# Fused scan and two MLPs on one core: the first two weight tiles in half-batches, a written-out order for the first block, attention loads on another queue

## Chip, cores, metric

The kernel runs on one core of a Trainium2 chip. The metric is the device time of one execution in microseconds (us); the outputs go back to HBM within it. Three runs of the kernel before gave 627.05, 629.52 and 629.43 us (median 629.43). One more execution, 627.23 us long, was recorded by the profiler; all rows below come from it.

## What is computed

```python
def _attn_ref(x, a, B, C):        # x (4, 8, 768, 32), a (4, 8, 768), B and C (4, 8, 768, 16)
    log_a = np.log(np.clip(a, 1e-06, 1.0))
    for c in range(nc):           # chunks along the sequence
        cum = np.cumsum(la, axis=-1)
        L = causal * np.exp(cum[:, :, :, None] - cum[:, :, None, :])
        M = np.einsum('bhin,bhjn->bhij', Cc, Bc) * L
        y[:, :, sl] = M @ xc + (Cc @ state) * np.exp(cum)[..., None]
        state = decay_full * state + sum_j(Bc x xc * decay_from_j)

def _moe_ref(x, w_gate, w_val, w_out, rms_g):       # x (3072, 256), d_ff 1536
    xn = x / np.sqrt(np.mean(x * x, axis=-1, keepdims=True) + 1e-06) * rms_g
    g = xn @ w_gate
    return (g / (1.0 + np.exp(-g)) * (xn @ w_val)) @ w_out

def _moe2_ref(x, w_in, w_out):                      # d_ff 2048
    h = x @ w_in
    return (h * np.clip(h + 3.0, 0.0, 6.0) / 6.0) @ w_out
```

A decayed linear attention over 4 batches feeds a normalised gated MLP, whose output feeds a second MLP. The MLP weights come in 64-bit floats, everything else in 32-bit.

## The kernel before, in words

**Tiles.** The sequence is cut into 6 blocks of 128 positions. A block holds the 4 batches: 4 "chunks" of 128 columns, 512 columns in all. Chunks are worked in pairs, q = 0 to 11; pairs 0 and 1 are the first block. Phase A runs the first MLP: 6 blocks times 12 weight tiles (`step`, f = 0 to 11). Phase B runs the second: 6 blocks times 16 weight tiles. Every product of two numbers is made from a high and a low part, as three matmuls (`mm3`, L829): high·high, low weight·high, high weight·low. So a step of phase A is two `hidden` groups of 6 matmuls of 512 columns (into `hps`), a `gate` on ScalarE (Silu, L862), a `prod` on VectorE (L870), a split into `gh` (ScalarE, L877) and `gl` (VectorE, L257), and one `result` group of 6 matmuls into `acc`. Two `hps` tiles and three each of `p`, `gh`, `gl` are in use in turn.

**Weights.** `weights` loads a tile of 64-bit numbers (768 KB) and turns it into `w1h` and `w1l`: two ScalarE passes (L772, L777), a VectorE join (L781), a cast to the high part (L261 or L263) and a VectorE subtraction (L257, `w1l`). Six staging buffers (`raw`) are used in turn. Every tile after the first also has a `hold`: a one-column GpSimd copy into the staging buffer (L975), which makes the tile's load wait for something earlier (`um` of chunk 1, or an earlier tile).

**Attention.** For each pair: loads of `cb` (all of C, B and x), of `L` (decays, spread to 64 partitions) and of `P` (prefix products); a VectorE scan of `L` (L454), products `bh` and `ch` (L257), then on TensorE `score` (L481) and `grow` (L492), on VectorE `SM` (L534), `um` (L540) and the state `V` (L548), then `intra` (L506) and `inter` (L515). ScalarE squares the result (L576). In the first block `L` and `P` are spread from SBUF by matmuls (L358, L364) with one-hot matrices `pick` and `eyeN`, which ScalarE copies out of the identity `eye` (L373, L379); GpSimd makes `eye8` and `eye`, in that order (L275 to L283). The norm of the first block is done for each pair (`norm_pair`): a mean by matmul (L597), a Sqrt on ScalarE (L629), a Newton step on VectorE (L610 to L612), a spread by matmul (L637), the scaling (L642) and the split of x into `xh` and `xl`. Later blocks use `norm` (L691 to L717), with a round trip through HBM (`rnd`, `rb`). Scores, products and sums of a pair lie in one PSUM tile, `sps`.

**Order.** Nothing is in program order. `Plan` collects operations with guessed durations, dependencies (`r`, `w`), pure order (`seq`) and a `boost`; `run` then simulates the engines and, whenever one is free, gives it the ready operation with the longest remaining path plus boost. Instructions are issued in the order so found, on one in-order queue for each engine. The place of an operation in the list decides only which buffers follow which. The first MLP step waits for all four batches (`xkeys[0]`). From the last mean of the first block until that step, `fill` puts matmuls on zeros (`idle`, L325) into gaps of TensorE, and `heat` runs six passes on zeros at the start (L351). All loads but four small or early ones go out on SyncE's queue (SP): weights (L763), `L` (L415), `cb` (L409), `P` (L424), the round trip of the norm (L709, L713).

Of the kernel before, what the change touches and what calls it, by code (L numbers as in the profile page):

```python
# [30 lines left out]
NWARM = (4, 4, 2)  # L31
VISITS = {0: [(0, 2, None), (2, 3, 2), (6, None, 3), (8,)],
# [3 lines left out]
class Plan:  # L36
# [9 lines left out]
    SLACK, BIAS = 400, 600  # L46
# [3 lines left out]
    def __init__(self, bufs):  # L50
        self.bufs, self.ops = bufs, []
        self.last, self.readers, self.users, self.first = {}, {}, {}, {}
        self.fill, self.pace, self.bytes, self.calm = None, {}, {}, 0

    def op(self, ns, fn, r=(), w=(), boost=0, seq=()):

        i, deps, order = len(self.ops), set(), set()
        ns = dict(ns)
        if "bytes" in ns:
            self.bytes[i] = ns.pop("bytes")  # L60
# [23 lines left out]

    def run(self):
# [22 lines left out]
        done, left, out = set(), set(), []  # L108
# [9 lines left out]
        while len(out) < len(ops):  # L118
# [21 lines left out]
            pri, i = now[e][0]  # L140

# [20 lines left out]
            if e == "POOL":  # L162
                free["DVE"] = max(free["DVE"], t) + self.SHARE * ops[i][0][e]
            land = end + self.LAT[e]
            if i in self.bytes:
                pipe = max(pipe, end) + self.bytes[i] / self.RATE
                land = pipe + self.LAND
            out.append((t, i, e))
            for s, full in succ[i]:
# [4 lines left out]
        out = [(t, i, lambda i=i, e=e: ops[i][1](e), ops[i][0][e] if e == "PE" else None)  # L174
               for t, i, e in out]
        if self.fill:
            fn, ns, after, cold, until = self.fill
            t = 1 + max(s for s, i, _, _ in out if i in after)
            cold += t
            for s, i, _, pe in sorted(o for o in out if o[3] is not None):  # L180
                while t + ns + self.SLACK < s:
                    out.append((t, -1, fn, None))
                    t += ns if t > cold else 2 * ns
                if i == until:
                    break
                t = max(t, s + pe)
# [5 lines left out]
def block_kernel(ctx, tc, comb, ablk, w1, w2, cst, out):  # L192
# [18 lines left out]
    ps_at = att.enter_context(tc.tile_pool(name="ps_at", bufs=1, space=PSUM, side="right"))  # L211
    ps_q = early[0].enter_context(tc.tile_pool(name="ps_q", bufs=1, space=PSUM))
# [15 lines left out]
    T = {}  # L228
# [6 lines left out]
    def dma(nbytes, n=1, e="DMA"):  # L235
        return {e: max(560 * n, nbytes // 370) if e == "DMA" else 560 * n, "bytes": nbytes}
# [32 lines left out]
    def setup():  # L269
# [4 lines left out]
        dve.memset(ac[:, 4], 1.0)  # L274
        pool.memset(eye8, 0.0)  # L275
        for base in (0, SC):
# [3 lines left out]
        pool.memset(ah, 0.0)  # L280
        pool.memset(eye, 0.0)
        pool.affine_select(out=eye, in_=eye, pattern=[[1, 128]], compare_op=ALU.not_equal,
                           fill=1.0, base=0, channel_multiplier=-1)  # L283

    P.op({"POOL": 2800}, lambda e: None, w=[("eye", 0)], boost=1e9)
# [12 lines left out]
    def clip_all(e):  # L298
        dve.tensor_scalar(out=az, in0=ac, scalar1=1e-6, scalar2=1.0, op0=ALU.max, op1=ALU.min)
        dve.tensor_copy(ah[:, :, 0:1], az[:, :, 0:1])  # L300
        dve.memset(az[:, :, 0:1], 0.0)
# [9 lines left out]
    def prefixes():  # L311
        P.op({"DVE": d2(320) + 280}, clip_all, r=[("ac", 0), ("ac", 1), ("eye", 0)], w=[("az", 0)], boost=1e5)
        P.op(dma(98304), lambda e: nc.sync.dma_start(out=rows(azero), in_=az[:, :4]), r=[("az", 0)],
             w=[("azero", 0)], boost=2e5)
        P.op({"DVE": ds(320)}, prefix, r=[("az", 0)], w=[("ac", 0), ("ac", 1)], boost=1e5)
# [8 lines left out]
    def idle():  # L324
        pe.matmul(out=bank4()[:, 0], lhsT=zero, rhs=four(zero), start=True, stop=True)  # L325


# [3 lines left out]
    def bank4(k=0):  # L331
        if ("ps", 0) not in T:
            T["ps", 0] = ps_at.tile([128, 4, 512], F32, name="sps")
        return T["ps", 1 if 2 <= k < B else 0]

    SCORE, Y, U = (0, 128), (256, 64), (384, 64)

# [756 lines left out]
```

## Time and profile before

| | |
|---|---|
| median of 3 runs (lowest, highest) | 629.43 us (627.05, 629.52) |
| profiled execution | 627.23 us |
| its span | 625.2 us |
| outside the span | 2.03 us |
| busy: TensorE, weight loads, VectorE, ScalarE, GpSimd | 610.8, 494.6, 388.5, 297.3, 6.9 us |

PE is TensorE, PEld its weight loads, DVE VectorE, ACT ScalarE, POOL GpSimd, SP SyncE; a "q" behind a name is that engine's queue of DMA issues. A busy time that is nearly the span names the busiest engine, not what each stage waits for; that is read from views of short stretches.

### The profile page before, as it was taken

The numbers are of one execution on the slowest core, as the hardware profiler recorded it, in microseconds if no ns is written. First come the engines' busy times: TensorE is split into PE (matmuls) and PEld (weight loads), VectorE is DVE, ScalarE is ACT, GpSimd is POOL, SyncE is SP. The second block draws the span as 40 slices with busy tenths as digits, with TensorE's granted clock in tenths as the row PEclk, the third lists the DMA queues.
The fourth block names the chain that finished last, engine by engine and source line by source line (L and its number), as shares of the span: only waits on it lengthen the run. The fifth ranks groups of instructions, "written<-read, shape, count | busy, mean of one in ns | idle before, by whom it ended". The sixth has DMA issues, their size and how long they took to land.

```text
span 625.2 us, 10728 instructions
## 1 busy us (share of the span) xinstructions
PE 610.8 (98%) x4442; PEld 494.6 (79%) x4442; DVE 388.5 (62%) x703; ACT 297.3 (48%) x501; POOL 6.9 (1%) x21
## 2 busy tenths in 40 slices
PE   7898999999999999999999999999999999999997
PEld 5576888788788778788888888888888888888886
DVE  6799988853793585566875455555555546454554
ACT  3687723232333323346765345454445445444543
POOL 1000000000000000000000000000000000000000
PEclk9799999999999999999999999999999999999999
DMA  5899205300420310023441000000000000000000
GB/s 199 312 240 332 71 18 144 106 15 18 145 61 0 103 61 17 2 91 129 147 150 41 1 0 1 1 35 1 1 35 0 0 35 1 18 17 0 35 1 35
DMA packets 15017, 40.89 MB, mean 65 GB/s; under 512 B 2084, under 2 KB 4856, under 8 KB 14968
## 3 DMA queue, kind: packets, MB, share of 16 engines
q1 hardware_dynamic: 14488, 39.24, 19.3%
q10 hardware_dynamic: 480, 0.96, 0.4%
q8 instruction: 35, 0.57, 0.4%
q14 instruction: 14, 0.11, 0.1%
HBM read 36.84 MB, written 3.35 MB: 64 GB/s over the span
## 4 chain that ended last, share of the span: by engine, by line
PE 91%; DVE 4%; DMA 3%; ACT 1%; issue 1%; SPq 0%; DVEq 0%
PE hps L829 48%; PE acc L829 36%; DMA cb<-comb 2%; DVE SM L534 1%; PE sps L506 1%; PE sps L481 1%; PE sps L515 1%; DMA P<-pref 1%; PE spread L351 1%; PE sps L492 1%; DVE L L454 1%; ACT sq L576 1%; PE sps L691 1%; PE spread L358 0%; DVE um L540 0%
## 5 line engine op out<-in xcount | busy, mean ns | idle before, releaser
L877 ACT CAST gh<-p 128x512 fp32r<-128x512 f32 x168 | 104.2, 621 | 149.8 <-PE acc L829 148.7
L257 DVE TENSOR_TENSOR gl<-p,gh 128x512 fp32r<-128x512 f32 x168 | 115.5, 688 | 78.0 <-ACT gh L877 77.9
L872 DVE SCALAR_TENSOR_TENSOR p<-p,hps 128x512 f32<-128x512 f32 x96 | 66.0, 688 | 71.9 <-ACT p L864 71.8
L864 ACT ACTIVATE p<-hps,half 128x512 f32<-128x512 f32 x96 | 66.1, 689 | 72.0 <-DVE gl L257 71.9
L829 PE MATMUL hps<-xh,w1h 128*128 128x512 f32 x288 | 90.7, 396 | 1.2 <-DVE p L870 0.7
L829 PE MATMUL hps<-xh,w1l 128*128 128x512 f32 x288 | 89.2, 391 | 0.5 <-DVE w1l L257 0.5
L829 PE MATMUL hps<-xl,w1h 128*128 128x512 f32 x288 | 88.8, 390 | 0.0
L829 PE MATMUL acc<-gh,w2h 128*128 128x512 f32 x192 | 74.7, 389 | 0.0
L829 PE MATMUL acc<-gh,w2l 128*128 128x512 f32 x192 | 74.7, 389 | 0.0
L829 PE MATMUL acc<-gl,w2h 128*128 128x512 f32 x192 | 74.7, 389 | 0.0
L870 DVE TENSOR_TENSOR p<-p,hps 128x512 f32<-128x512 f32 x72 | 49.3, 685 | 35.0 <-PE hps L829 27.6
L862 ACT ACTIVATE p<-hps 128x512 f32<-128x512 f32 x72 | 43.0, 597 | 48.4 <-DVE gl L257 24.8
L829 PEld LDWEIGHTS hps<-xh,w1h 128*128 128x128 f32 x288 | 52.9, 188 | 14.3 <-DVE p L870 1.3
L829 PEld LDWEIGHTS hps<-xh,w1l 128*128 128x128 f32 x288 | 53.8, 188 | 13.0 <-DVE w1l L257 1.7
L829 PEld LDWEIGHTS hps<-xl,w1h 128*128 128x128 f32 x288 | 54.0, 188 | 11.7 <-issue 0.2
L829 PE MATMUL hps<-xh,w2l 128*128 128x512 f32 x192 | 59.1, 389 | 0.0
L829 PE MATMUL hps<-xl,w2h 128*128 128x512 f32 x192 | 59.1, 389 | 0.0
L829 PE MATMUL hps<-xh,w2h 128*128 128x512 f32 x192 | 59.1, 389 | 0.0
L829 PE MATMUL acc<-gh,w1h 128*128 128x512 f32 x144 | 56.5, 392 | 0.0
L829 PE MATMUL acc<-gh,w1l 128*128 128x512 f32 x144 | 56.1, 389 | 0.0
L829 PE MATMUL acc<-gl,w1h 128*128 128x512 f32 x144 | 56.0, 389 | 0.0
L829 PEld LDWEIGHTS acc<-gh,w2l 128*128 128x128 f32 x192 | 36.0, 188 | 7.5
(106 smaller groups left out, 638.7 us busy)
## 6 DMA issues: line engine op xcount, KB each, us to landing
cb<-comb SPq DMA_DIRECT2D x10, 896.0 KB
raw<-w SPq DMA_DIRECT2D x16, 512.0 KB
L<-azero SPq DMA_DIRECT2D x20, 256.0 KB
yT<-w SPq DMA_DIRECT2D x6, 768.0 KB
rawx<-w SPq DMA_DIRECT2D x6, 768.0 KB
out<-yT SPq DMA_DIRECT2D x12, 256.0 KB
P<-pref SPq DMA_DIRECT2D x20, 64.0 KB
rb<-rnd SPq DMA_DIRECT2D x5, 256.0 KB
```

The lines of the kernel that those rows point to most:

```text
L257: eng[e].tensor_tensor(out=out, in0=a, in1=b, op=op)
L351: pe.matmul(out=Q[3][:, :128 * n], lhsT=zero, rhs=four(zero, n), start=True, stop=True)
L454: dve.tensor_tensor_scan(out=L, data0=Q[k] if k < B else L, data1=flat(eye8), initial=0.0, op0=ALU.mult, op1=ALU.add)
L481: pe.matmul(out=o[64 * c:64 * c + 64, p], lhsT=cb[r, BN + c * SC:BN + (c + 1) * SC], rhs=cb[r, CP + c * CH:CP + (c + 1) * CH], start=True, ...
L492: pe.matmul(out=o[32 * p:32 * p + 32, c], lhsT=b[r, 32 * p:32 * p + 32], rhs=cb[r, XX + 64 * p:XX + 64 * p + 64], start=False, stop=True, ...
L506: pe.matmul(out=y[32 * g:32 * g + 32, 2 * t + c], rhs=SM[r, h], lhsT=cb[r, XX + D * h:XX + D * h + D], start=first, stop=True, skip_group_ ...
L829: pe.matmul(out=o, lhsT=a, rhs=c, start=first and i == 0, stop=last and i == len(seq) - 1)
L862: act.activation(out=p[:, :n], in_=hid(hs[0])[:, :n], func=AF.Silu)
L864: act.activation(out=p[:, :n], in_=hid(hs[0])[:, :n], func=AF.Relu, scale=1.0 / 6.0, bias=half)
L870: dve.tensor_tensor(out=p, in0=p, in1=h, op=ALU.mult)
L872: dve.scalar_tensor_tensor(out=p, in0=p, scalar=1.0, in1=h, op0=ALU.min, op1=ALU.mult)
L877: act.copy(out=t[:, :n], in_=T["p", i][:, :n])
```

## The change

- The first two weight tiles (`NE = 2`) are run for the first block in two half-batches of 256 columns: batches 0 and 1 (pair 0) with f = 0 and 1, then batches 2 and 3 (pair 1) with f = 0 and 1; from f = 2 on all 512 columns as before. In a half step both hidden groups share one `hps` tile. A gate now also waits for the Silu table.
- `chain` writes out the order of the first block on VectorE, ScalarE and TensorE.
- `spot` and `each` go from ScalarE to VectorE; GpSimd makes `eye` first; `heat` makes two matmuls (four passes) where it made three; `fill` and `idle` are gone.
- `L`, `cb` and `P` of all pairs from 2 on are issued by GpSimd. Only f = 3 keeps a `hold` (on `um` of chunk 3); later tiles come after it in order.
- `sps` tiles are marked (`ps=`), so that the planner keeps an engine off one that another engine still uses; the two PSUM pools swap places, so that the first pair's tile is freed first.
- The `VISITS` of block 0 move down the list; some guessed durations change.

```diff
-NWARM = (4, 4, 2)
-VISITS = {0: [(0, 2, None), (2, 3, 2), (6, None, 3), (8,)],
+NWARM = (4, 4)
+NE = 2
+VISITS = {0: [(3, 2, None), (5, 3, 2), (8, None, 3), (9,)],
...
+    def chain(self, e, tags):
+        at = [self.named[t] for t in tags.split()]
+        for i in at:
+            for o in [o for o in self.ops[i][0] if o != e]:
+                del self.ops[i][0][o]
+        for a, b in zip(at, at[1:]):
+            if a not in self.ops[b][2]:
+                self.ops[b][3].add(a)
...
+            who, until = owner.get(self.held.get(i), (e, 0))
+            if who != e and until > t:
+                heapq.heappop(now[e])
+                heapq.heappush(future[e], (until, i))
+                continue
...
-        if self.fill:
-            fn, ns, after, cold, until = self.fill
...
         def ld_cb2(e):
-            (act if e == "ACT" else nc.sync).dma_start(
+            pool.dma_start(
...
         def ld_L(e):
-                nc.sync.dma_start(
+                pool.dma_start(
...
         def ld_P(e):
-                nc.sync.dma_start(out=t[:, i], in_=src.to_broadcast([H, N, CH]))
+                pool.dma_start(out=t[:, i], in_=src.to_broadcast([H, N, CH]))
...
-        seq = [("raw", 2)] if q == B // 2 else []
+        seq = [("raw", 3)] if q == B // 2 else []
...
-    def step(ph, b, f, n, acc):
-        i = nxt(nstep)
+    def step(ph, b, f, n, acc, q=None):
+        i, o = nxt(nstep), 256 * (q or 0)
...
+        if q is not None:
+            P.op({"PE": 2 * mmc}, lambda e: [hidden(e, v) for v in range(2)],
+                 r=wk + xk + [("open", 1)], w=hs)
...
-            if v == 0:
-                P.op({"ACT": a1(n)}, gate, r=[hs[0]], w=[("p", i)])
+        P.op({"ACT": a1(n)}, gate, r=[hs[0]] + ([("table", 0)] if A else []), w=[("p", i)])
...
     def hold(f):
-        g = max(f - 2, 0) + (f == 2)
...
-            s = flat(T["um", 1]) if f == 1 else raw1(g)[:, 1:]
-            pool.tensor_copy(t[:, :1], s[:, :1])
-        return (go, [("um", 1) if f == 1 else ("raw", g)]) if f else ()
+            pool.tensor_copy(t[:, :1], flat(T["um", 3])[:, :1])
+        return (go, [("um", 3)]) if f == 3 else ()
...
-                seq=[("azero", 0)], hold=hold(f))
+                seq=[("azero", 0)] + ([("raw", 3)] if f > 3 else []), hold=hold(f))
...
-            step("A", xb[j], f, B * CH, acc)
+            if j or f >= NE:
+                step("A", xb[j], f, B * CH, acc)
+            elif f == 0:
+                for q in range(2):
+                    for g in range(NE):
+                        step("A", xb[j], g, 256, acc, q)
...
+    P.chain("DVE", "spot0 spot1 spot2 spot3 clip each prefix scan0 bh0 scan1 bh1 ch0 ch1 SM0 SM1 um0 "
+            "um1 scan2 scan3 bh2 bh3 ch2 ch3 wj0 v0 iv0 nw0 SM2 SM3 um2 um3 sx00 sx01 wl0 xl0 wj1 "
+            "v1 iv1 nw1 wl1 sx10 sx11 xl1")
+    P.chain("ACT", "P0 P1 wa0 sq0 sq1 wb0 rt0 ev0 ev1 wa1 wh0 xh00 xh01 wb1 sq2 sq3 wh1 rt1 ev2 ev3 "
+            "silu xh10 xh11")
+    P.chain("PE", "heat sp0 sp1 sc0 sc1 px gr0 gr1 sp2 sp3 visit0 mn0 mn1 sc2 sc3 gr2 gr3 bk0 visit1")
```

In the chains `sp` is the spreading matmul of a chunk, `sc` score, `gr` grow, `mn` mean, `bk` the spread of the norm, `wa`, `wb`, `wj`, `wh`, `wl` the five passes of a weight tile, `sq` square, `rt` root, `ev` evacuation, `v`, `iv`, `nw` the norm's VectorE work, `sx` the scaling, `xh` and `xl` the split of x.

## Rows read from the trace of the kernel before

**Rows 1.** The page: span, and busy time of each engine.

```profile
span 625.2 us, 10728 instructions
...
PE 610.8 (98%) x4442; PEld 494.6 (79%) x4442; DVE 388.5 (62%) x703; ACT 297.3 (48%) x501; POOL 6.9 (1%) x21
```

**Rows 2.** The stretches: PE, PEld, DVE, ACT, POOL busy (instructions); PEclk; DMA.

```profile
19.70:22.40 2.70, 2.46 (x15) 2.46 (x12) 1.63 (x4) 0.66 (x2) 0.00 (x0) 0.50 0.96 378
22.40:26.30 3.90, 3.90 (x9) 1.95 (x9) 2.47 (x10) 3.01 (x8) 0.70 (x2) 0.50 1.01 393
26.50:29.90 3.40, 3.40 (x14) 2.09 (x12) 2.17 (x5) 3.40 (x7) 0.14 (x1) 1.00 0.91 343
29.90:33.00 3.10, 2.15 (x8) 1.22 (x8) 3.06 (x5) 3.10 (x6) 0.37 (x1) 1.00 1.05 226
33.00:58.50 25.50, 22.76 (x393) 17.10 (x392) 23.66 (x43) 19.47 (x31) 2.37 (x5) 1.00 0.92 272
58.50:87.80 29.30, 29.30 (x141) 23.87 (x142) 28.65 (x52) 18.21 (x30) 0.00 (x0) 1.00 0.30 99
```

**Rows 3.** The chain that ended last: start, us, what.

```profile
26.89 13.58 DMA cb<-comb
40.49 4.95 DMA P<-pref
...
77.31 5.44 PE hps L829 x24
...
82.75 1.36 PE acc L829 x6
```

**Rows 4.** PE by line from 26.74 to 58.5; hps and acc first of three.

```profile
L829 PE MATMUL hps<-xh,w1h 128*128 128x512 f32 x27 | 9.2, 418 | 1.2 <-DVE p L870 0.7 <-DVE w1h L263 0.5
...
L506 PE MATMUL sps<-SM,cb 64*32 64x64 f32 x128 | 1.8, 224 | 1.5 <-DVE um L540 1.5
...
L829 PE MATMUL acc<-gh,w1h 128*128 128x512 f32 x4 | 1.6, 389 | 0.0
```

**Rows 5.** Timeline of the first block: start, us, engine, line.

```profile
1.05 4.63 PE L351 MATMUL spread<-zero 128*128 128x512 f32 x6 [1.05 <-DVE zero L270]
...
6.78 2.34 DVE L454 TENSOR_TENSOR_SCAN L<-spread,eye 128x512 f32<-128x512 f32 x2 [1.24 <-PE spread L358]
...
13.37 0.26 DVE L540 TENSOR_TENSOR um<-sps,gs 128x128 f32<-128x128 f32 x1
...
16.36 0.97 PEld L597 LDWEIGHTS sps<-ones,sq 128*128 128x128 f32 x8
...
18.30 0.70 PEld L506 LDWEIGHTS sps<-SM,cb 64*32 64x32 f32 x64 [0.97 <-DVE um L540]
...
24.44 1.28 ACT L966 ACT_TABLE_LOAD   x1
...
25.47 1.50 PE L325 MATMUL sps<-zero 128*128 128x512 f32 x2
...
26.74 0.83 PE L829 MATMUL hps<-xh,w1h 128*128 128x512 f32 x2
...
27.06 0.69 DVE L257 TENSOR_TENSOR xl<-xT,xh 128x512 fp32r<-128x512 f32 x1 [0.28 <-ACT xh L261]
...
32.20 0.82 ACT L261 CAST w1h<-yT 128x768 fp32r<-128x768 f32 x1
...
74.40 1.28 DVE L257 TENSOR_TENSOR xl<-xT,xh 128x512 fp32r<-128x512 f32 x2
```

**Rows 6.** Loads issued by SP, and a GpSimd copy beside VectorE: timeline.

```profile
30.30 0.33 SPq L763 DMA_DIRECT2D yT<-w  x1
...
36.75 4.32 SPq L424 DMA_DIRECT2D P<-pref  x2
...
50.21 0.95 DVE L781 SCALAR_TENSOR_TENSOR yT<-yT 128x768 int32<-128x768 int32 x1
...
50.31 0.89 POOL L975 COPY rawx<-yT 128x1 f32<-128x1 f32 x1 [2.48 <-DVE V L548]
```

More of the change, by code (lines that the diff above doesn't have):

```diff
@@ L107, in run @@
         free = dict.fromkeys(self.ENGINES, 0)
-        done, left, out = set(), set(), []
+        done, left, out, owner = set(), set(), [], {}
         pipe = 0
@@ L173, in run @@
                     enter(s)
-        out = [(t, i, lambda i=i, e=e: ops[i][1](e), ops[i][0][e] if e == "PE" else None)
-               for t, i, e in out]
-        if self.fill:
-            fn, ns, after, cold, until = self.fill
[L178 to L186, printed above, removed]
+        out = [(t, i, lambda i=i, e=e: ops[i][1](e)) for t, i, e in out]
         for o in sorted(out, key=lambda o: o[:2]):
@@ L274, in setup @@
         dve.memset(ac[:, 4], 1.0)
+        dve.memset(az[:, :, 0:1], 0.0)
+        pool.memset(eye, 0.0)
+        pool.affine_select(out=eye, in_=eye, pattern=[[1, 128]], compare_op=ALU.not_equal,
+                           fill=1.0, base=0, channel_multiplier=-1)
+        pool.memset(ah, 0.0)
         pool.memset(eye8, 0.0)
@@ L322, in four, with bank4, held @@
         return t.rearrange("p (o n) -> p o n", o=1).to_broadcast([128, n, 128])
-    def idle():
-        pe.matmul(out=bank4()[:, 0], lhsT=zero, rhs=four(zero), start=True, stop=True)
     CT, BN, CP, XX, BT, CW = 0, 128, 256, 512, 768, 896
[L331 to L334, printed above, removed]
+    def bank4(k=B):
+        return T["ps", held(k)]
     SCORE, Y, U = (0, 128), (256, 64), (384, 64)
+    def held(k):
+        return min(k // 2, 1)
     def part(k, at):
@@ new lines, in spot @@
+            for r in (2 * k, 2 * k + 1):
+                dve.tensor_copy(pick[:, r:r + 1], at[:, r:r + 1].to_broadcast([96, 1, 2, SC]))
+        for k in range(B):
+            P.op({"DVE": 400}, lambda e, k=k: spot(k), r=[("eye", 0)],
+                 w=[("pick", k) if k else ("raw", 4)], boost=2e6 - 1e5 * k, tag=f"spot{k}")
+        P.op({"PE": 3500}, heat, w=[("hot", 0)], boost=1e9, tag="heat")
+        P.op({"DVE": 350}, each, r=[("eye", 0)], w=[("raw", 5)], seq=[("az", 0)], boost=1e5, tag="each")
@@ L603, in rn, with guess, newton @@
         return T["rn", j]
-    def newton(j, a, b, keys, bst, ns=570):
+    def guess(j, a, b):
+        v, y, z = (t[:, a:b] for t in rn(j))
+        dve.tensor_scalar(out=z.bitcast(I32), in0=v.bitcast(I32), scalar1=1, scalar2=None,
+                          op0=ALU.logical_shift_right)
+        dve.tensor_scalar(out=y.bitcast(I32), in0=z.bitcast(I32), scalar1=-1.0,
+                          scalar2=float(0x5F3759DF), op0=ALU.mult, op1=ALU.add)
+    def newton(j, a, b, keys, bst, ns=570, tag=None):
         v, y, z = keys
@@ L883, in result @@
         def result(e):
-            if f == 0:
+            if f == 0 and not q:
                 for a in acc:
@@ L889, in result @@
                 c = oo + 128 * m
-                mm3(T["acc", a][:, :n], [wh[:, c:c + 128]], [wl[:, c:c + 128]],
-                    [T["gh", i][:, :n]], [T["gl", i][:, :n]], f == 0, f == nf - 1)
+                mm3(T["acc", a][:, o:o + n], [wh[:, c:c + 128]], [wl[:, c:c + 128]],
+                    [T["gh", i][:, :n]], [T["gl", i][:, :n]], f == 0 and not q, f == nf - 1)
         if i:
@@ L1007, in go @@
                 inter(k)
[L1009 removed]
+        P.op({"PE": 2700 if new and old else 1100 if new else 1600}, go, r=r, w=w, boost=BOOST, ps=0)
         for k in old:
```

188 lines of the change are left out of this document (90 added, 98 removed).

## The prediction

> **What bounds the kernel now.** I read the page first, then the stretches, then the chain and the first block's timeline. TensorE is busy for 610.8 of 625.2 us [rows 1], so nearly all of the span is matmuls that the change keeps. What can move is the head and the time that TensorE loses before it is dense. The stretches show where that is: from 29.90 to 33.00 it is busy 2.15 of 3.10 us, from 33.00 to 58.50 22.76 of 25.50, and from 58.50 on all the time [rows 2]. ScalarE is full from 26.50 to 33.00, VectorE nearly so from 29.90 to 87.80. The chain says what came late in 27 to 58 us: a `cb` transfer of 13.58 us, and a `P` transfer of 4.95 behind it, then VectorE work; from 58.50 on it is matmuls only [rows 3].
>
> How much TensorE loses there has a floor and a ceiling. The floor is the idle time, 0.95 + 2.74 = 3.7 us [rows 2]. A matmul of 512 columns in a dense run takes 1.36 / 6 = 0.227 us [rows 3]. From 26.74 to 58.50, 31.8 us, there are 27 + 26 + 26 into `hps` and 3 times 4 into `acc`, 91 in all, so 20.6 us; with 1.8 us of `intra` [rows 4] that leaves 9.3, in which the other attention matmuls must still fit. I take **5 us lost**, nearer the floor.
>
> The head is a chain through all engines. `heat` ends at 5.68, the first scan starts at 6.78, the `um` of chunk 1 at 13.37, `intra` of the second pair at 18.30, and `xl` of the second pair ends at 27.75. The first MLP matmul is at 26.74, for all four batches [rows 5].
>
> **The change, part by part.** The sum is against the profiled execution: 625.2 + 2.03 outside the span = 627.23 us.
>
> *Head, first pair.* `heat` is 4.63 us for ten parts of 128 columns [rows 5] and keeps eight of them, so it ends 0.9 us earlier, and the spreading matmuls and scans follow. The chain runs both `grow` before the third and fourth spread, and `um` of chunk 1 before the third scan of 1.17 us [rows 5]; so `um` 1, at 13.37 now, comes some 2 us earlier. `spot` and `each`, nine copies, fall to VectorE while it waits for `a` and just behind `clip`: nothing. The Newton step of pair 0 now comes before `SM2`, about 1 us, which uses up half of those 2 us for pair 1. I estimate that `intra` of pair 1 and its `xl` stay within 0.7 us of 18.30 and 27.75, and count nothing for it.
>
> *Half steps.* The first pair's x is due at about 20 to 21 us by this reckoning, so 24 matmuls of 256 columns can run before the second pair's x. A 256-column matmul costs half of 0.227, or the load of its weights if that is longer: eight loads of 128 columns took 0.97, so 0.121 each [rows 5]. I take 0.12. That moves 24 × 0.12 = **2.9 us** out of the dense part. Nothing is the least, all 36 of the pair (`result` too), 4.3, the most. I take 24, because the gates wait for the Silu table, loaded at 24.44 for 1.28 us now [rows 5] and still last but two in ScalarE's chain. Behind that wait stand the third and fourth half steps, which need the two `hps` tiles back; so they start about when the second pair's x is there, which costs nothing more. The halves themselves cost 72 × (0.121 - 0.113) = **+0.5**.
>
> *Weights.* Tile 1 is converted during the head rather than at 27 to 31 us, so the 0.95 us idle from 29.90 to 33.00 [rows 2] should go: **-1.0** (0 at least). Tile 2's cast, at 32.20 now [rows 5], comes no sooner, since ScalarE also has four half gates and splits; TensorE has the four results and two half steps to do until then.
>
> *Loads.* Ten of the eleven GpSimd copies go, and with them the waits of the weight loads on SP; tiles 1 and 2 are loaded in the head. `L`, `cb` and `P` of pairs 2 and 3 (ten issues) stand behind the one copy left, which waits for `um` 3 at about 18.3, and in GpSimd's own order. No row shows a load issued by GpSimd. SP takes 0.33 us for a weight tile and 4.32 / 2 = 2.16 for a `P` [rows 6]; a GpSimd copy that met a VectorE instruction took 0.89 us and ended with it [rows 6], so 2.16 + 0.95 = 3.1 is the far end. I take 1.5, between them, so the last `P` leaves at 33.5, well ahead of 45.44, where it landed [rows 3]. Then the two transfers in the chain no longer decide; VectorE is next, busy 23.66 of 25.50 us there [rows 2], so of the 4 us lost from 33 to 58.5 I let half go: **-2.0** (0 to -4).
>
> The Trainium skill, "DMA: Bandwidth & Descriptors", section "Issuing engines are not separate DMA queues", says that loads of all issuers share the same 16 engines and that a second issuer saves only issue time. By that rule the 13.58 us would stay, and the sum would be 2.0 higher; the trace bears it out in part, with a DMA share of 1.01 at 22.40 to 26.30, but 0.92 later and 0.30 from 58.5 on [rows 2].
>
> *Clock.* TensorE ran at half (0.50, so 1.2 GHz) from 19.70 to 26.30, and at 2.4 GHz from 26.50 on [rows 2]. Before the rise it was busy without a gap, with zeros from `fill` among that (1.50 us at 25.47 [rows 5]). Without `fill` the half steps must do it. At the low level the early 2.9 us take 5.8, which still fits into 20 to 26.7. If the rise comes a little later, some dense work runs at half: **+0.5** (0 to half of 6.6 = 3.3).
>
> *The rest.* `ps=`, `VISITS` and guessed durations only move entries of the plan: a visit shares no buffer with a step, so its place in the list orders nothing. SP's norm round trips lose neighbours on their queue, but they are not in the chain. From 58.5 to 87.8 TensorE has no idle time to win [rows 2]. Nothing, ±1.
>
> Sum: -2.9 + 0.5 - 1.0 - 2.0 + 0.5 = -4.9, so 622.3 us. Two of the three runs lie 2.2 us above the profiled execution; I add half of that, 1.1: **623.4 us**, 1.0% below the median.
>
> **The rivals.**
>
> *A: conversion stays the bound.* ScalarE is full from 26.50 to 33.00 [rows 2]. If the half gates push tile 2's conversion back, the work done early only becomes a wait for tile 2. Terms 2.9 and 1.0 go, 0.5 of halves and half a us of clock stay, so -2.0 + 1.0 = -1.0: 626.2, or 627.3 on the runs' scale. For it: both engines full. Against it: tile 1 is already out of the way, worth about 2.6 us of ScalarE (three passes near the 0.82 of [rows 5]).
>
> *B: GpSimd issues slowly, slower than before.* VectorE is busy over 90% from 29.90 on, and a GpSimd copy waited out a whole VectorE instruction [rows 6]. If each step of an issue does that, a load takes several us, the ten come one after another, and block 1's x comes late. It was split by 75.7 [rows 5]. TensorE asked for it at 77.31 + 3 × 1.36 = 81.4 (13 `hidden` groups by 58.5, eight more to 77.31, then four in that row [rows 3]), with the change at 76.5, and holds five `result` groups, 6.8 us, back to fill in. With issues of 5 us `P` lands at 68.5, 23 later than 45.4, x at 98.7, and TensorE stands 98.7 - 76.5 - 6.8 = 15.4: 637.7, or 638.8. It decides from 3.9 us an issue, where the stall eats the 4.9. Against it: the copy reads SBUF, an issue need not, and 3.1 is the most that the rows make likely.
>
> The Trainium skill, "SBUF — State Buffer", section "SBUF: two separate sides", warns of this trap: while VectorE is in a two-port mode, GpSimd can't write descriptors. By its section "Who interferes with whom", instructions with two SBUF inputs stop only GpSimd work that reads SBUF, and the trace agrees as far as it goes: 0.89 us beside such an instruction.
>
> *C: the clock stays low.* If, without `fill`, dense work runs 6.6 us at half, 3.3 us are lost, not 0.5: 625.1, or 626.2. For it: four matmul groups with gaps are thinner than zeros. Against it: at half speed they take twice the time.
>
> *D: the halves do nothing.* If the first pair's x comes no earlier than the second's, term 2.9 is 0: 625.2, or 626.3. I count this into A.
>
> **How the numbers follow.** Forecast 0.60, A with D 0.18, C 0.12, B 0.10. A difference of 0.5%, about what can be told here, is 3.1 us: faster is under 626.3. Of A and C, which lie around that, a fifth (0.06) falls below: faster 0.66, same 0.24, slower 0.10 (B). The low end takes all lost time and all 36 matmuls: -4.3 + 0.5 - 1.0 - 4.0 = -8.8, 618.4, with 1.1 for scale 619.5, less 1 for the rest: 618.5. The high end is A with 1 for the rest and 1.1 to the upper runs: 629.4. B and a little at each end stay out, 2 in 10.
>
> **What would show it.** Right: the first `hps` matmuls, of 256 columns, at 19.5 to 21.5 us; Silu gates not before 25; no idle TensorE from 27 to 33; `P` of pair 3 landed before 40; idle TensorE from 33 to 58 about half of 2.74. Wrong: `hps` waiting for `w1h` of tile 2 (A); loads by GpSimd over 3 us apart and `score` waiting for them (B); PEclk 0.50 beyond 28 us (C); or new gaps after 58.5.

## The result: 622.11 us, and the profile of the changed kernel

Four runs of the changed kernel took 624.2, 621.74, 621.43 and 622.47 us, median **622.11 us**; the kernel before, four runs beside them, 629.47. The ratio is 0.9897 with a 95% interval of 0.9863 to 0.9931, so 6.5 us less (4.3 to 8.6). The forecast was 623.4 in a range of 618.5 to 629.4. The profiled execution is the slowest of the four, 624.2 us, with 622.4 of span. One more set of runs of the same kernel (the first experiment) gave 621.32 in the median and a profile of 621.49 us; I call it the repeat and use it where the two differ. The profiled execution of the kernel before, 627.23 us, is 1.0 to 2.2 us below the medians of its groups, so the profiles can place 5.5 us at most of the 6.5 to 6.9 that the medians show.

The page of the changed kernel, span and busy times, against [rows 1]:

```profile
span 622.4 us, 10795 instructions
...
PE 610.3 (98%) x4472; PEld 499.4 (80%) x4472; DVE 386.8 (62%) x707; ACT 296.9 (48%) x505; POOL 33.6 (5%) x61
```

TensorE's busy time hardly moved, 610.8 to 610.3 us. GpSimd now counts 33.6 us, of which 12.5 + 10.7 + 7.5 = 30.7 are issues of loads (last section); the profile records them as work. Line numbers have moved: `intra`, `inter`, square, copy and the norm's sum stand at L515, L524, L586, L271 and L705, where they were L506, L515, L576, L261 or L263, and L691.

The stretches of the changed kernel, columns as in [rows 2]:

```profile
22.40:26.30 3.90, 2.06 (x11) 1.98 (x11) 1.65 (x7) 1.95 (x5) 0.48 (x1) 0.50 1.01 245
26.50:29.90 3.40, 3.40 (x18) 3.40 (x18) 2.87 (x6) 2.11 (x6) 0.00 (x0) 0.50 1.03 393
29.90:33.00 3.10, 3.10 (x20) 3.10 (x20) 2.72 (x5) 2.33 (x6) 0.00 (x0) 0.65 1.02 258
33.00:58.50 25.50, 23.39 (x413) 18.84 (x412) 23.56 (x45) 20.62 (x34) 3.52 (x6) 1.00 1.02 302
```

Two things are to be seen. The granted clock is 0.50 (1.2 GHz) where it was 1.00 before, from 26.50 to 29.90, and 0.65 after that. And TensorE is idle 25.50 - 23.39 = 2.11 us from 33.00 to 58.50, against 2.74 before, of which 1.99 us are one stop in the middle of an `intra`, behind its 33rd matmul:

```profile
57.03 0.46 PE L515 MATMUL sps<-SM,cb 64*32 64x64 f32 x31 [1.99 <-issue]
```

The repeat stops behind the same matmul of the same group, but for 0.46 us only:

```profile
54.69 0.46 PE L515 MATMUL sps<-SM,cb 64*32 64x64 f32 x31 [0.46 <-issue]
```

"issue" says that the profile finds no engine, transfer or semaphore that ended the stop (the last section has more on it). The two profiled executions differ by 2.7 us. Their idle time from 33.00 to 58.50 differs by 2.11 - 0.96 = 1.15 us. The rest is mostly ahead of 33 us, where the first profile had begun `hps` matmuls worth 22 of 512 columns and the repeat 27, which is 5 × 0.227 = 1.1 us. The repeat's granted clock was higher in all three stretches:

```profile
22.40:26.30 3.90, 2.25 (x16) 2.16 (x16) 1.64 (x7) 2.71 (x6) 1.19 (x2) 0.88 1.03 267
26.50:29.90 3.40, 3.40 (x19) 3.40 (x19) 3.30 (x8) 2.74 (x7) 0.00 (x0) 0.53 1.02 368
29.90:33.00 3.10, 3.10 (x23) 2.92 (x23) 3.10 (x6) 2.34 (x7) 0.00 (x0) 0.96 1.02 309
```

Now the part that no row ahead of the prediction covers; first the kernel before, 87.80 to 330.00:

```profile
87.80:330.00 242.20, 239.82 (x2262) 194.46 (x2261) 158.76 (x319) 99.24 (x177) 0.00 (x0) 1.00 0.24 78
```

Then the repeat:

```profile
33.00:58.50 25.50, 24.54 (x428) 19.26 (x427) 23.89 (x46) 22.07 (x37) 3.61 (x6) 1.00 1.02 315
87.80:330.00 242.20, 241.48 (x2271) 196.04 (x2270) 157.73 (x313) 104.32 (x194) 18.43 (x30) 1.00 0.25 79
```

From 87.80 to 330.00 TensorE was idle 242.20 - 239.82 = 2.38 us before and 0.72 after. No term of the prediction was drawn from this stretch. With it all but 0.2 us of the difference of the two spans, 625.2 - 619.7 = 5.5 us, has a place:

- by 33 us: the columns of the `hps` and `acc` matmuls begun are worth 19 matmuls of 512 columns before and 27 in the repeat; 8 at 0.227 us [rows 3] are 1.8 us;
- 33.00 to 58.50: 2.74 - 0.96 = 1.8 us less idle time;
- 87.80 to 330.00: 2.38 - 0.72 = 1.7 us less.

The head, in the timeline of the changed kernel, against [rows 5]:

```profile
1.06 3.78 PE L362 MATMUL spread<-zero 128*128 128x512 f32 x4 [1.06 <-DVE zero L280]
...
10.56 0.48 DVE L549 TENSOR_TENSOR um<-sps,gs 128x128 f32<-128x128 f32 x2
...
17.58 1.18 PE L515 MATMUL sps<-SM,cb 64*32 64x64 f32 x64 [0.31 <-DVE um L549]
...
19.63 0.66 ACT L586 ACTIVATE sq<-sps 128x256 f32<-128x256 f32 x2
...
19.81 0.77 PE L837 MATMUL hps<-xh,w1h 128*128 128x256 f32 x2 [0.24 <-DVE xl L267]
...
22.51 1.70 PE L607 MATMUL sps<-ones,sq 128*128 128x1 f32 x8
...
25.28 0.95 DVE L267 TENSOR_TENSOR w1l<-yT,w1h 128x768 fp32r<-128x768 f32 x1
...
26.05 1.22 PE L652 MATMUL sps<-eye,y 128*128 128x128 f32 x4 [1.84 <-ACT xT L271]
...
26.92 0.78 PE L837 MATMUL hps<-xh,w1h 128*128 128x256 f32 x2
27.42 0.37 ACT L872 ACTIVATE p<-hps 128x256 f32<-128x256 f32 x1
...
28.98 0.68 DVE L267 TENSOR_TENSOR xl<-xT,xh 128x512 fp32r<-128x512 f32 x1
```

The first MLP matmul, of 256 columns, starts at 19.81, where it was 26.74. But only one half step (12 matmuls) runs then. The mean of the second pair stands behind it on TensorE's queue: the squares are there at 20.3, the mean begins at 22.51. The second half step begins at 26.92, behind the spread of the norm, and `xl` of the second pair ends at 28.98 + 0.68 = 29.66, later than the 27.75 of before.

### The profile page after: what moved, and what is told of

Read it like the earlier page. It is cut to its first block, busy times and chain, and to the rows that moved or that the text cites. A ratio compares the mean times of both kernels' runs of the same rounds, so it can differ in the third digit from the quotient of the medians.

```text
span 622.4 us, 10795 instructions
## 1 busy us (share of the span) xinstructions
PE 610.3 (98%) x4472; PEld 499.4 (80%) x4472; DVE 386.8 (62%) x707; ACT 296.9 (48%) x505; POOL 33.6 (5%) x61
## 4 chain that ended last, share of the span: by engine, by line
PE 94%; DVE 4%; issue 1%; DMA 1%; ACT 0%; SPq 0%; DVEq 0%; ACTq 0%
PE hps L837 52%; PE acc L837 36%; PE sps L515 1%; PE sps L524 1%; PE sps L490 1%; PE sps L501 1%; PE spread L362 1%; DMA rb<-rnd 1%; DVE L L462 0%; DVE yT L788 0%; DVE SM L543 0%; PE sps L705 0%; DVE xl L267 0%; DVE w1l L267 0%; PE sps L607 0%
## 5 line engine op out<-in xcount | busy, mean ns | idle before, releaser
L887 ACT CAST gh<-p 128x512 fp32r<-128x512 f32 (+1 forms) x170 | 104.5, 616 | 147.1 <-PE acc L837 145.8
L267 DVE TENSOR_TENSOR gl<-p,gh 128x512 fp32r<-128x512 f32 (+1 forms) x170 | 115.8, 681 | 78.7 <-ACT gh L887 78.5
L837 PE MATMUL hps<-xh,w1h 128*128 128x512 f32 (+1 forms) x296 | 92.8, 396 | 0.4 <-DVE xl L267 0.2
L837 PE MATMUL hps<-xh,w1l 128*128 128x512 f32 (+1 forms) x296 | 91.1, 390 | 0.0
L837 PE MATMUL hps<-xl,w1h 128*128 128x512 f32 (+1 forms) x296 | 90.9, 389 | 0.0
L880 DVE TENSOR_TENSOR p<-p,hps 128x512 f32<-128x512 f32 (+1 forms) x74 | 49.6, 670 | 49.8 <-PE hps L837 43.1
L872 ACT ACTIVATE p<-hps 128x512 f32<-128x512 f32 (+1 forms) x74 | 43.3, 585 | 52.3 <-PE hps L837 26.7
L837 PE MATMUL acc<-gh,w1h 128*128 128x512 f32 (+1 forms) x148 | 57.5, 388 | 0.0
L837 PE MATMUL acc<-gh,w1l 128*128 128x512 f32 (+1 forms) x148 | 56.8, 384 | 0.0
L837 PE MATMUL acc<-gl,w1h 128*128 128x512 f32 (+1 forms) x148 | 56.8, 384 | 0.0
```

The costliest lines, as they stand in the source:

```text
L267: eng[e].tensor_tensor(out=out, in0=a, in1=b, op=op)
L837: pe.matmul(out=o, lhsT=a, rhs=c, start=first and i == 0, stop=last and i == len(seq) - 1)
L872: act.activation(out=p[:, :n], in_=hcols(0), func=AF.Silu)
L880: dve.tensor_tensor(out=p, in0=p, in1=h, op=ALU.mult)
L887: act.copy(out=t[:, :n], in_=T["p", i][:, :n])
```

## The experiments

All runs of a group stood beside runs of the kernel before on the same chip; ratios are to those. The first repeats the change; the next seven leave one part of it out, put one back, or change the head; the last four follow from what the run without marks showed. The repeat stood only beside the first group (the change again to the filler); for the others the ratios compare best.

**The change again.** No edit.

> The changed kernel itself, once more, as the yardstick of this group and for a second profile. Forecast: 620.5 to 624 us, 0.986 to 0.993 of before. In the first profile TensorE stood at half clock from 15 to 32 us, and stood still 2.0 us in the middle of one intra group (55.04 to 57.03) with nothing to release it. If that stall is an accident of that execution, the second profile lacks it and its span is 1.5 to 2.5 us shorter at the same clock; if the kernel causes it, it is there again at the same instruction.

Measured: 621.32 us (621.01 to 621.95), ratio 0.989 (0.9873 to 0.9907); the kernel before 628.24. This is the zero line for the next three. The stop is there again at the same instruction, so the kernel has a part in it, but it is 0.46 us long and not 2.0.

**Without half steps.**

```diff
-NE = 2
+NE = 0
```

> The change without half-batches (NE = 0): the first two weight tiles run on all 512 columns, the rest as changed. Theory H (the half steps carry the gain): about 2.5 us slower than the changed kernel, 624 to 626 us, first hps matmul not before 26. Theory L (the loads and the written-out order carry it): within 1 us of the changed kernel, since the second pair's mean no longer queues behind the first half step (in the profile 22.5 us, while its squares were ready at 20.3), so the second pair's xl ends near 27.5 rather than 29.7 us.

Measured: 622.66 us (622.07 to 627.98), ratio 0.9922 (0.9894 to 0.995). The half steps are worth 1.3 us by the medians and 2.0 by the ratios, whose intervals overlap. The clock stays at 0.50 here too, until about 30 us:

```profile
26.50:29.90 3.40, 3.01 (x7) 2.42 (x8) 2.85 (x4) 3.13 (x6) 0.00 (x0) 0.50 1.01 375
```

so the half steps aren't what keeps it low.

**Loads back on SyncE.** `L`, `cb` and `P` of pairs 2 and on are issued by SP as before, with the guessed costs of before; the holds stay gone.

```diff
-            pool.dma_start(
+            nc.sync.dma_start(
...
```

> The change with L, cb and P of pairs 2 to 11 issued by SyncE again, with the planner's costs of before; all else as changed (the holds stay gone). Theory L: 2 us slower than the changed kernel, 623.5 to 626 us, with transfers of cb and P back in the chain before 58 us. Theory H: within 0.7 us. A third outcome: it is the missing holds, not the issuer, that let the loads go early; then also within 0.7 us, but cb of pair 2 lands before 32 us all the same.

Measured: 623.61 us (622.66 to 624.38), ratio 0.9922 (0.9906 to 0.9938): 2.3 us slower than the repeat, and no run of one overlaps a run of the other. The chain of this kernel shows the way of it:

```profile
22.62 15.34 DMA L<-azero
...
38.02 13.13 DMA rawx<-w
```

An `L` load and a weight load, one behind the other on SP's queue, last from 22.62 to 51.15 us. The chain of the changed kernel has no load between 20 and 66 us.

**A filler for the clock.** A matmul on zeros, 512 columns, stands between mean and spread of the second pair, where TensorE is idle.

```diff
+    P.op({"PE": 1900}, zfill, r=[("open", 1)], w=[("acc", 0)], boost=BOOST0, tag="zfill")
...
-    P.chain("PE", "heat sp0 sp1 sc0 sc1 px gr0 gr1 sp2 sp3 visit0 mn0 mn1 sc2 sc3 gr2 gr3 bk0 visit1")
+    P.chain("PE", "heat sp0 sp1 sc0 sc1 px gr0 gr1 sp2 sp3 visit0 mn0 mn1 sc2 sc3 gr2 gr3 bk0 visit1 mn2 mn3 zfill bk1")
```

> The change with one matmul on zeros (512 columns, into an accumulator tile that the first result overwrites) between the mean and the spread of the second pair's norm, where TensorE stood idle from 24.2 to 26.05 us. Theory C (a good part of the head start is lost because dense work runs at half clock until 32 us): the clock rises at 25 to 29 us and 1.5 to 2.6 us are saved, 618.5 to 621 us. Rival: the second pair's x, not TensorE's speed, sets the pace until 33 us; then within 0.7 us of the changed kernel, although the clock rises earlier.

Measured: 621.44 us (621.26 to 621.59), ratio 0.989 (0.9874 to 0.9907), the repeat's own. The clock did what it should:

```profile
26.50:29.90 3.40, 2.77 (x21) 2.40 (x21) 3.40 (x8) 3.39 (x8) 0.00 (x0) 1.00 1.00 395
```

It is 1.00 in the stretch where the first profile has 0.50 and the repeat 0.53, and TensorE is busy 2.77 us there instead of 3.40 in both. VectorE and ScalarE are both full: TensorE got faster and waited for them instead. So the low clock of the repeat in these 3.4 us costs nothing that can be measured. The run does not say what the longer low stretch of the first profile cost, since the repeat did not have that.

**Without the PSUM marks.** The planner again doesn't know that an engine still uses an `sps` tile.

```diff
-            self.held[i] = ps
+            pass
```

> The change without the marks on the PSUM tiles (the planner no longer keeps an engine off a tile that another one uses); all else as changed. Theory M: the marks took away waits after 58.5 us that the prediction counted as nothing. In the kernel before, TensorE waited 1.5 us in three places there for um before the norm's sums; in three profiles with the marks it waits in none, and its lead over the kernel before grows by 2 us between 85 and 300 us. Then 1.3 to 2.2 us slower than the changed kernel, 622.6 to 623.6 us, with such waits back. Rival (the lead there comes from the loads, which no longer stand behind each other on SP): within 0.6 us.

Measured: 626.83 us (626.07 to 627.29), ratio 0.9974 (0.996 to 0.9987). Of the 6.9 us of the repeat 1.6 are left. **The marks are worth 5.5 us (628.93 × (0.9974 - 0.989) = 5.3 by the ratios), which my prediction had put at nothing.** The stretch beyond 87.80 us:

```profile
87.80:330.00 242.20, 239.21 (x2258) 193.67 (x2257) 160.32 (x321) 103.68 (x185) 18.44 (x30) 1.00 0.26 80
```

TensorE is idle 2.99 us in it, 2.3 more than in the repeat. The rest of what the marks are worth lies ahead of it: 1.1 us more idle time from 33.00 to 58.50 (table below), and by 33 us `hps` matmuls worth 20.5 of 512 columns, where the repeat had begun 27 (1.5 us).

**Without the written-out order.** The three `chain` calls are taken out.

```diff
-    P.chain("DVE", ...)
-    P.chain("ACT", ...)
-    P.chain("PE", ...)
```

> The change without the three written-out orders: the planner orders the first block itself. Theory O (the written-out order brings the first pair's x forward, without it the half steps gain nothing): first hps matmul later by 1.5 us or more, and 1 to 2.5 us slower, 622.3 to 624 us. Rival (the planner finds nearly the same order; what the order gives the first pair it takes from the second): within 0.7 us.

Measured: 621.81 us (621.39 to 622.2), ratio 0.9903 (0.9883 to 0.9922). No difference from the changed kernel that these intervals can tell.

**The first half step in two.** Its two `hidden` groups become two operations, with the mean of the second pair between them.

```diff
-            P.op({"PE": 2 * mmc}, lambda e: [hidden(e, v) for v in range(2)],
+            P.op({"PE": mmc}, lambda e: hidden(e, 0), r=wk + xk + [("open", 1)], w=hs, tag=f"ha{q}{f}")
+            P.op({"PE": mmc}, lambda e: hidden(e, 1), r=wk + xk + [("open", 1)] + hs, w=hs, tag=f"hb{q}{f}")
...
-... gr3 bk0 visit1")
+... gr3 bk0 visit1 ha00 mn2 mn3 hb00 bk1")
```

> The change with the first half step's two hidden groups apart and the second pair's mean between them, in a fixed order on TensorE. In the changed kernel that mean waits behind 12 matmuls (its squares are ready at 20.3, it starts at 22.5). Theory X (until 33 us the second pair's x sets the pace): mean and x of the second pair come 1 to 1.5 us sooner and 0.5 to 1.2 us are saved, 620 to 620.8 us. Rival (the conversion of weights on ScalarE and VectorE sets it): within 0.4 us of the changed kernel, although x is sooner.

Measured: 621.21 us (620.8 to 621.93), ratio 0.9894 (0.9875 to 0.9914). No difference: that the mean stands behind a half step is seen in the timeline, but it costs nothing that these runs can tell.

**Tile 1's low part earlier.** In VectorE's chain `wl1` goes ahead of the norm of the second pair, so that the second half step needn't wait for it.

```diff
-            "v1 iv1 nw1 wl1 sx10 sx11 xl1")
+            "wl1 v1 iv1 nw1 sx10 sx11 xl1")
```

> The change with tile 1's low part (wl1) ahead of the second norm in VectorE's written-out order, where VectorE stands idle for 3.5 us (21.1 to 24.5) in front of it. The second half step can then run at 24.2, in TensorE's idle time. Theory X (the second pair's x sets the pace): the spread of its norm moves behind those 12 matmuls, x comes 1 us later, within 0.6 us of the changed kernel or slower. Rival (the early work counts): 0.5 to 1.4 us saved, 620 to 620.8 us.

Measured: 622.57 us (621.74 to 623.66), ratio 0.9917 (0.9897 to 0.9936), some 1 us slower in the median than the two runs before it, though the intervals of the ratios overlap, so that "not better" is all that is sure. The second half step does start earlier (24.78); the price comes behind it:

```profile
22.40:26.30 3.90, 3.90 (x20) 3.90 (x20) 1.75 (x7) 1.98 (x5) 1.12 (x2) 0.50 1.04 265
26.50:29.90 3.40, 2.04 (x10) 1.74 (x9) 2.24 (x5) 2.26 (x6) 0.00 (x0) 0.69 0.99 367
29.90:33.00 3.10, 1.62 (x10) 1.62 (x11) 3.10 (x7) 2.15 (x6) 0.00 (x0) 0.84 1.05 316
```

TensorE is full to 26.30 and then idle 1.36 + 1.48 us, since the spread of the second pair's norm now stands behind both half steps (27.48, where it was 26.05), and the third half step waits for a `p` whose gate comes after that pair's x on ScalarE.

**The marks alone, in the kernel before.** The `ps=` of every operation and the test in `run` go into the kernel before; nothing else does.

```diff
+            who, until = owner.get(self.held.get(i), (e, 0))
+            if who != e and until > t:
+                heapq.heappop(now[e])
+                heapq.heappush(future[e], (until, i))
+                continue
...
-        P.op({"ACT": a1(256)}, square, r=[yk], w=[("sq", j, i)], boost=bst)
+        P.op({"ACT": a1(256)}, square, r=[yk], w=[("sq", j, i)], boost=bst, ps=held(k))
...
```

> The kernel before with the PSUM marks alone. Theory (the marks carry most of the gain by themselves, since without them the changed kernel lost 5.5 us): 4 to 5.5 us under the kernel before, near 624. Rival (they only give back what the new order of the first block would otherwise lose): within 1.5 us of the kernel before. In both the waits of VectorE's SM for ScalarE's square, 11.3 us in seven from 33 to 330 us before, should fall to some 7 or less.

Measured: 625.45 us (623.98 to 626.89), ratio 0.9942 (0.9925 to 0.9959), so 3.6 us (2.6 to 4.7). That is nearer the theory's 4 to 5.5 than the rival's 1.5, though below it. VectorE's waits for ScalarE on `sps` came out as both had it, 7.0 us. The idle time went where the theory says:

```profile
87.80:330.00 242.20, 241.48 (x2269) 195.88 (x2268) 155.15 (x311) 102.39 (x190) 0.00 (x0) 1.00 0.26 79
```

0.72 us, as in the changed kernel, while the 22.97 busy us from 33.00 to 58.50 are nearly those of before.

**Marks on the first block only.** `SM`, `um`, square and copy of later blocks, the visits and the sums of the norm are left unmarked.

```diff
+    def mark(k):
+        return held(k) if k < B else None
...
-w=[("sq", j, i)], boost=bst, ps=held(k), tag=f"sq{k}")
+w=[("sq", j, i)], boost=bst, ps=mark(k), tag=f"sq{k}")
...
```

> The changed kernel with marks on the first block's operations only. Theory (the marks pay in the later blocks, where the lead over the kernel before is lost between 85 and 400 us without them): 625 to 627, close to the run without any marks. Rival (they pay in the first block): 621 to 622.5.

Measured: 627.61 us (626.46 to 630.47), ratio 0.9991 (0.9976 to 1.0006): nothing of the gain is left that can be told from zero. The theory's 625 to 627 was a little too kind.

**Marks on the later blocks only.** The other half: later blocks as in the change, no marks on the first block's operations.

```diff
+    def mark(k):
+        return held(k) if k >= B else None
...
```

> The changed kernel with marks on the later blocks only. Theory (as for the run with marks on the first block only): 621.3 to 622.5, the whole gain. Rival: 625 to 627. If both halves of the marks are needed, both runs come out between.

Measured: 622.19 us (621.19 to 622.81), ratio 0.989 (0.9872 to 0.9908): all of the gain, as the theory said. The marks pay in the later blocks and, as far as these runs can tell, nowhere else.

**Visits under the same mark.** In the change the visits, the norm's sum and its shift have mark 0, while `SM`, `um`, square and copy of later blocks have mark 1. So for later blocks the marks keep VectorE and ScalarE off each other, and TensorE only off that shift. Here all have 1.

```diff
-        P.op({"PE": 2700 if new and old else 1100 if new else 1600}, go, r=r, w=w, boost=BOOST, ps=0)
+        P.op({"PE": 2700 if new and old else 1100 if new else 1600}, go, r=r, w=w, boost=BOOST, ps=1)
...
```

> The changed kernel with the visits, the sums and the shift of the norm under the same mark as the SM, um, square and copy of the later blocks (they stand under another one, so that the marks keep only VectorE and ScalarE off each other). Theory (it is the turn between VectorE and ScalarE that pays, and TensorE's visits are ordered by their data already): within 1 us of 621.5. Rival (TensorE in turn too would be better, or would hold VectorE back): more than 1 us away, on either side.

Measured: 622.85 us (621.59 to 625.7), ratio 0.9914 (0.989 to 0.9937). The median is 1.35 us above 621.5, so just on the rival's side, but the interval overlaps that of the change: nothing is settled but that it isn't better. TensorE's turn is not what pays.

The idle time of TensorE in the profiles, from the stretches as above (length less PE busy), sorts the runs:

| us idle | 33.00 to 58.50 | 58.50 to 87.80 | 87.80 to 330.00 | ratio |
|---|---|---|---|---|
| before | 2.74 | 0.00 | 2.38 | 1 |
| marks alone | 2.53 | 0.29 | 0.72 | 0.9942 |
| all but the marks | 2.07 | 0.00 | 2.99 | 0.9974 |
| marks on the first block only | 2.45 | 0.57 | 2.95 | 0.9991 |
| marks on later blocks only | 0.11 | 0.00 | 0.72 | 0.989 |
| visits under the same mark | 0.20 | 0.00 | 1.68 | 0.9914 |
| the change (repeat) | 0.96 | 0.06 | 0.72 | 0.989 |

The third column goes with the later blocks' marks: 0.72 with them as in the change, 2.38 to 2.99 without, whatever else is there. With the visits under the same mark it is 1.68, of which 1.0 us is a single wait for a `p` of ScalarE.

**What the marks do.** One norm of a later block shows it. The timeline of the kernel before, from the `inter` of its last pair to the sum of the squares (`L691`), the work on `sps`:

```profile
111.73 0.69 PE L515 MATMUL sps<-ch,V 32*64 32x64 f32 x32
112.49 0.38 ACT L576 ACTIVATE sq<-sps 128x256 f32<-128x256 f32 x1 [2.15 <-PE sps L515]
112.90 0.76 DVE L263 COPY xT<-sps 128x256 f32<-128x256 f32 x2 [1.44 <-ACT sq L576]
113.69 0.39 ACT L576 ACTIVATE sq<-sps 128x256 f32<-128x256 f32 x1 [0.82 <-DVE xT L263]
...
115.94 0.64 PE L691 MATMUL sps<-sq,ones 128*32 128x128 f32 x16 [0.57 <-DVE um L540]
```

The same place in the repeat of the changed kernel:

```profile
107.99 0.69 PE L524 MATMUL sps<-ch,V 32*64 32x64 f32 x32
...
108.75 0.66 ACT L586 ACTIVATE sq<-sps 128x256 f32<-128x256 f32 x2 [2.16 <-PE sps L524]
109.29 0.66 ACT L271 COPY xT<-sps 128x256 f32<-128x256 f32 x2
...
111.61 0.64 PE L705 MATMUL sps<-sq,ones 128*32 128x128 f32 x16
```

Before, the second square stood 0.82 us behind VectorE's copies, though both only read the tile: the two engines take turns on it. The old planner did not know that. It gave VectorE the copies (`evac` may run on either engine), as if they could run beside the squares, and the plan's order then made each engine stand for the other with its whole queue behind it. With the marks the plan sees the tile taken and gives the copies to ScalarE, which has it already: two squares and two copies without a gap. From `inter` to the sum it took 4.21 us before and 3.62 after, and TensorE's wait of 0.57 us at the sum is gone. The groups of the copies between 87.80 and 330.00 say the same for all of them. Before:

```profile
L263 DVE COPY xT<-sps 128x256 f32<-128x256 f32 x8 | 3.0, 420 | 5.5 <-ACT sq L576 5.5
L261 ACT COPY xT<-sps 128x256 f32<-128x256 f32 x8 | 2.8, 379 | 3.0 <-DVE SM L534 2.3 <-DVE um L540 0.7
```

After:

```profile
L271 ACT COPY xT<-sps 128x256 f32<-128x256 f32 x16 | 5.3, 394 | 0.0
```

Eight copies on each engine, with 8.5 us of standing, became sixteen on ScalarE with none. The waits of the two kernels from 33 to 330 us (us in total, times, longest), first before, the longest of those between the two engines on `sps` and the one of TensorE:

```profile
DVE SM L534 <- ACT sq L576: 11.3, 7, 3.2
...
DVE xT L263 <- ACT sq L576: 5.5, 4, 1.4
...
ACT sq L576 <- DVE xT L263: 3.3, 4, 0.8
ACT xT L261 <- DVE SM L534: 3.2, 4, 1.0
ACT sq L576 <- DVE SM L534: 3.0, 4, 0.8
...
PE sps L691 <- DVE um L540: 1.5, 3, 0.6
```

After, the only row of this kind between the two engines is:

```profile
DVE SM L543 <- ACT xT L271: 6.7, 4, 2.7
```

The Trainium skill, "PSUM — Partial Sum Buffer", section "Terms", says that no two engines may be on the same bank and quadrant at once, reads against reads included, so that an order between them is needed even where data asks for none. The waits above agree: those of VectorE and ScalarE for each other are between two readers. No run here shows what would happen without the order.

## Why the number was right and its reasons were not

The forecast of 623.4 was 1.3 us above the median, but two errors cancelled, and that is luck.

**The step that failed is "The rest ... Nothing, ±1"**, and in it the sentence that `ps=` "only move entries of the plan". Moving entries is what a plan does to time: the marks are worth 5.5 us with the rest of the change there, 3.6 without it. The two grounds given for nothing were true where I looked and did not reach far enough. TensorE has no idle time from 58.5 to 87.8, and the chain from 58.50 on showed matmuls [rows 2, 3]; but no term came from beyond 87.80, where it lost 2.38 us. The trace of the kernel before shows the loss, 1.46 us of it from 100 to 200 us:

```profile
100.00:200.00 100.00, 98.54 (x905) 80.05 (x904) 66.09 (x139) 32.77 (x59) 0.00 (x0) 1.00 0.22 68
```

So do the three waits of TensorE for `um` at the norm's sums (1.5 us, above), and so does the page: span less PE busy is 625.2 - 610.8 = 14.4 us [rows 1], of which the floor had counted 3.7. Nor did the miss lie in that stretch alone. Some 2.3 us of what the marks are worth are there; the others are ahead of 87.80, in stretches whose idle time I had counted, but put down to other causes.

**The terms that I did count were too large together.** All of the change but the marks is worth 1.6 us (0.8 to 2.5), where their sum was 4.9. With the marks in place the same parts are worth 3.3 (625.45 with marks alone, 622.19 with the rest and the later blocks' marks, same group of runs). So 6.9 - 3.6 - 1.6 = 1.7 us come from both being there, though by the intervals of the four ratios that is only about as large as its uncertainty. The profiles put most of it ahead of 87.80: by then `hps` and `acc` matmuls worth 215 of 512 columns had begun before, 216 with the marks alone, 221 with all but the marks, and 232 in the repeat. So the marks win next to nothing there by themselves and 11 matmuls, 2.5 us, with the rest. Why is not shown, and these are single executions: the first profile of the changed kernel, marks and all, has 221.

The sum held one term more, the 1.1 us for executions that are slower than the profiled one. The changed kernel shows none of it: the median of the repeat, 621.32, lies at its profiled execution, 621.49. On the profile's scale the sum said 622.3, and 621.5 was measured.

- *Head.* `heat` ends at 4.84, 0.84 earlier; `um` of the first pair is 2.6 us earlier (I said some 2); `intra` of pair 1 is at 17.58, 0.72 before 18.30 (I said within 0.7). `xl` of pair 1 was to stay within 0.7 us of 27.75 and is 1.9 late (29.66), since the mean of the second pair stands behind the first half step at half speed. That queueing I had not costed; the split half step shows no cost of it.
- *Half steps.* Net -2.4 was forecast; 1.3 was measured (2.0 by the ratios). The mis-sized term is "I take 24": 12 matmuls ran ahead of the old start, not 24, which makes 12 × 0.12 = 1.4. The next half step waited for tile 1's `w1l`, at 25.28 in VectorE's chain behind the norm's step that waited for ScalarE, and for the spread ahead of it on TensorE. Running 24 early, as tile 1's low part earlier did, was no better.
- *Weights.* The idle time from 29.90 to 33.00 went, as said, 0.95 to 0.00 us, and nothing waits for tile 2. At the low clock this stretch holds less work than its busy time says, and no run took this term alone.
- *Loads.* -2.0 forecast, 2.3 measured by putting them back; but the way was another. An issue was taken at 1.5 us and was 0.54 to 0.75 (below); the 2.16 for a `P` on SP was a misreading of [rows 6], where 4.32 us hold two issues of 0.58 and SP's wait between them. And the last `P` of pair 3 had left at 21.64 + 1.24 = 22.88 where I had said 33.5. (Not all ten issues stood behind the one copy left: pair 2's `P` went ahead of it, at 14.91.) The rule of the Trainium skill that I weighed, "DMA: Bandwidth & Descriptors", section "Issuing engines are not separate DMA queues" (a second issuer saves only issue time), would have left this term out. The engines are shared, as it says: the DMA share from 33.00 to 58.50 is 1.02 here and 0.98 with the loads on SP, and the loads of pair 3, though issued so early, landed at about the old times. `cb` landed at 20.6 + 21.5 = 42.1 us (40.47 before) and the last `P` at 22.3 + 21.9 = 44.2 (45.44 before). Still the kernel with the second issuer is 2.3 us faster. By the chain with the loads on SP, what it gains is that loads and weights no longer stand in one line; no run parts that from the time of issuing that SP saves.
- *Clock.* +0.5 was forecast for a late rise. In the first profile it rose after 29.90, where it had risen by 26.50; that was the sign I had set for rival C, and by 33 us this execution is 1.1 us of matmuls behind the repeat. In the repeat the low 3.4 us cost nothing that the filler run can tell: its faster TensorE waits 0.35 + 0.27 us there for the second pair's x. So C's 3.3 us were too many; whether 0.5 was right is not shown.
- *The rivals.* A needed `hps` to wait for tile 2: no such wait is in the profile. B decided at 3.9 us an issue: 0.54 to 0.75. C: above. D: the halves do something, 1.3 us.
- *The signs.* First `hps` at 19.81 (19.5 to 21.5 said), the first gate at 27.42 (not before 25), no idle TensorE from 27 to 33: right. Idle time from 33 to 58.5 was to be about half of 2.74, 1.37: 2.11 in the first profile, 0.96 in the repeat. `P` of pair 3 landed at 44.2 and not before 40: wrong. None of these signs would have told that the larger part of the gain lay elsewhere.

What stays open: what the stops inside `intra` wait for; how much of the gain the earlier tile 1 has; and whether the interplay of 1.7 us is one.

## What to carry to other kernels

Before an edit to a scheduler is put at nothing, add up the idle time of the bounding engine over the whole span, stretch by stretch, and ask which of it that edit could touch; a wrong zero hides in what no term covers. Tell a planner about every resource on which engines must take turns, a shared PSUM tile among them, and let the engine that holds a tile finish with it (squares and copies together), rather than splitting the reads over two engines. And take parts away one at a time and put them in one at a time: here the marks are worth 3.6 us alone and 5.5 with the rest, and a total that fits proves none of its terms.

## What the runs showed of the hardware

GpSimd's issues of loads, over the whole changed kernel (count, busy us, mean ns, idle before):

```profile
L432 POOL DMA_DIRECT2D P<-pref x20 | 12.5, 627 | 75.1 <-DVE V L557 61.7 <-ACT z L644 11.3 <-DVE ch L267 1.8
L423 POOL DMA_DIRECT2D L<-azero x20 | 10.7, 539 | 50.3 <-DVE um L549 32.3 <-DVE SM L543 17.7 <-issue 0.2
L417 POOL DMA_DIRECT2D cb<-comb x10 | 7.5, 753 | 60.8 <-PE sps L515 60.8
```

0.54, 0.63 and 0.75 us each, and the six issues of 33.00 to 58.50 take 3.52 us in all beside a VectorE that is busy 23.56 of 25.50. The warning of the Trainium skill, "SBUF — State Buffer", section "SBUF: two separate sides", that VectorE can keep GpSimd from writing descriptors while it is in a two-port mode, shows no cost in these issues; whether an instruction of that mode ran beside one of them is open.

TensorE can run at 1.2 GHz at no loss while it is not what the rest waits for: from 26.50 to 29.90 the granted clock was 0.53 in the repeat and 1.00 in the filler run, and the two took the same time to 0.1 us.

TensorE can stop between two matmuls of one group with nothing that the profile names as the cause. An `intra` between 47 and 59 us does so in five of the profiled executions: for 1.99 us in the first profile, 0.39 and 0.46 in the repeat, 0.89 with the filler, 0.78 with the marks alone, 0.27 and 1.20 with marks on the first block only. Ahead of each of the seven stops one packet moved on the queue that the profile calls `instruction`, and it was done 1.3 to 1.7 us before the matmuls went on. In the first profile it lies between 54.3 and 55.6 us (packets, MB, share):

```profile
q8 instruction: 1, 0.02, 6.0%
```

That TensorE waits there for its own instructions would fit, but no run tried it, and the other profiles have such packets at about the same times without a stop. What is shown is that the stop of one kernel varied from 0.46 to 1.99 us, so that a single profile can be 0.2% off by it.
